# Reworked start, last 64 columns of the third layer on two column groups, and two more transposes on TensorE, in a convolution-and-MLP kernel written out task by task

## The chip, the cores and the metric

The kernel runs on one core of one Trainium2 chip. The metric is the device time in microseconds (us). Three runs of the kernel before took 302.81, 300.95 and 302.58 us; their median is 302.58 us. A core has a matrix engine (TensorE, PE in the profile; PEld is its loading of weights), VectorE (DVE), ScalarE (ACT), GpSimd (POOL), SyncE (SP, which here only issues transfers), and 16 DMA engines. Matmul results land in PSUM, from where VectorE or ScalarE copy them to SBUF ("eviction").

## The reference

One batch of S = 2048 positions with D = 640 channels; all inputs are bfloat16. `LN` is a layer norm without weights.

```
sa, ca, ga, sb, cb, gb = split(silu(c) @ w_mod)          # six vectors of 640
h   = LN(q) * (1 + ca) + sa
ksh = sum over t = 0..3 of shift(k, t) * shift_k[:, 3-t]  # causal, per channel
kv  = ksh * v
y   = irfft(rfft(kv, 4096) * rfft(ssm_k, 4096))[:2048] + kv * ssm_D
x   = q + ga * (h * y)
h   = LN(x) * (1 + cb) + sb
h1  = gelu(LN(h) @ w1)                                    # w1: 640 x 640
hs  = (quarters of h1 shifted by 1, -1, 2, -2 positions) @ w2
x1  = h + hs
x   = x + gb * (x1 + gelu(LN(x1) @ w3) @ w4)             # w3: 640 x 1728
```

## The kernel before, in words

**A plan written out by hand.** The body calls `add(engine, cost, function, r=..., w=...)` 1046 times. Each call records one task: a few instructions, with the regions of SBUF that it reads and writes, from which the dependences follow. The string `ORDER` (line 26 on) then lists each task by number with a letter for its engine (P, A, D, G, S for PE, ACT, DVE, POOL, SP) and, for tasks that take PSUM, the slot. `Planner.run` goes through this list, and each engine executes its tasks strictly in the listed order. The costs given to `add` play no part in the order; some tasks allow two engines, and the letter in `ORDER` decides. A transfer is issued by the queue that its letter names, in the order of that queue, so a transfer that must wait holds up those listed behind it.

**The front (0 to about 8 us).** `ssm_D`, `ssm_k` (five transfers of 128 channels, 512 KB each, into `Ra`, L228), `shift_k` and `c` are loaded in this order on SP. `ssm_D`, `shift_k` and `c` come with the channel on the partition: `Dcol` (L226), `skT` (L229) and `c_col` (L230), where `Dcol` and `c_col` are filled element by element, two bytes each. k and v come transposed by DMA (L233). VectorE computes index columns in sixteen tiny steps (`scol`, L262 to L279). Tables of sines follow: GpSimd makes an integer ramp, VectorE multiplies it by an index column (L292) and takes it modulo the period (L293), and ScalarE applies the sine (`sin_to`, L321); a second table goes through GpSimd (`angles_pool`, `turns_to`). L332 and L333 finish the matrix `F1bd`, L348 writes a negated part of the table `RG`, and SP copies parts of it to other partitions (L353, L354). GpSimd builds diagonal matrices from the taps of `shift_k` into `RQ` (L355) and computes silu of `c` (L380 on).

**Transforms (8 to about 110 us).** The long convolution is a Fourier transform of length 4096, split into 64 x 64. L444 adds `Dcol` to the first tap of `ssm_k` in `Ra`, `to_slots` (L394) transposes 32 x 32 blocks on VectorE, `stage1` (L407) multiplies by `F1bd` on TensorE, and its results are evicted by ScalarE (L207) or VectorE (L209). `stage2` (L427) is the second transform. The same is done for kv, after `k_shift` (L463, L468), which runs on the diagonal matrices. The modulation vectors come from w_mod (L487 to L510). `inverse1` multiplies the two spectra. For that it needs a copy with real and imaginary parts exchanged: four such "swap" buffers `KSY` are used in turn, each filled by transfers on SP and GpSimd (L613), read by VectorE (L617), and followed by matmuls (L628, L629). L576 copies a table from `RK` to `RH`. `inverse2` (L661) is the last transform, 32 x 32 tiles of the array, sixteen at a time.

**Layers (110 us to the end).** The positions are held as sixteen tiles A of 128. The groups of the first layers are `CG` = [0], [1], [2], then pairs [3,4] to [13,14], then [15]; those of the later layers are `MG` = [1], then pairs [2,3] to [14,15], then [0]. For each group:

- `chain_a` (L737, L740): gate times convolution, residual sum, and a square sum on ScalarE (L729) for the variance; `ln_finish` turns sums into mean and scale on GpSimd (L714 to L717), its first part on VectorE where `ORDER` says so.
- `chain_b` (L751, L756): modulation, and statistics of the next norm.
- `chain_c`: the norm itself (`normed`, L724 for the first groups, L592/L594 otherwise), then `turn`, which brings channels onto partitions: for the first `pe_c = 4` groups (tiles 0 to 4) with five transposes on TensorE (L772) and an eviction by ScalarE or VectorE (L778, L780), for the later ones by a transposing DMA on SP (L765). `pe_m = 3` says the same for the groups of the later layers.
- `mm_w1`: first layer (L818), gelu (L820), and its remaining 32 channels of each quarter (L828, gelu in four pieces on ScalarE, L834).
- `mm_w2`: mixing matmul (L873), residual on VectorE (L880), square sum, norm, turn.
- `mm_w3`: third layer (L907). The 1728 columns of w3 are 13 blocks of 128 and 64 left over. SBUF holds the left-over 64 twice (L1020, a copy on GpSimd), as a fourteenth block of 128 columns; so TensorE computes 14 blocks per group, in tasks of 4, 4, 4 and 2, each block five matmuls with the group's 128 or 256 positions as moving columns. gelu follows (L911).
- `mm_w4`: fourth layer (L937), 13 blocks whole, and the half block with `half` (L928): four matmuls of 64 rows each, two at a time on the two row groups of the array. The first tile uses the upper copy, the second the lower copy of the doubled 64.
- VectorE adds residuals and multiplies by gb (L960 to L966), and SP sends the output (L969).

The weights w1 and w2 are loaded at L992 to L995, w3 at L1012, w4 at L1014 and L1009/L1010, all on SP.

## Time and profile before

| view | value |
|---|---|
| median of three runs | 302.58 us |
| span of the profiled execution | 298.7 us |
| what lies around the span, taken from the median | 302.58 - 298.7 = 3.9 us |
| mean granted TensorE clock | 0.975 |
| TensorE matmuls, busy | 269.7 us, 90%, 3176 instructions |
| TensorE weight loads, busy | 208.5 us, 70% |
| VectorE, busy | 218.2 us, 73% |
| ScalarE, busy | 208.3 us, 70% |
| GpSimd, busy | 104.8 us, 35% |
| DMA | 35.76 MB in 58356 packets |

The profile is of one execution, and its rows are measured from the start of the span. The page gives no total for that execution besides its span, so the difference to the runs' median stands in the table as one term. Busy shares are means over stages: TensorE's 90% contains a stretch at the start where it has nothing to do and long stretches with no gap. The views used below are: the span cut into windows with the busy time of each engine; an engine's waits, each with the tile or line for which it waited (`PE ps_w L873 <- ACT R L820: 2.1, 1, 2.1` means that TensorE's matmuls of L873 waited in total 2.1 us, once, at longest 2.1 us, for ScalarE's L820); the timeline of one engine (start, duration, instruction, and in brackets the idle time before it with what ended it); the costliest groups of instructions; the transfers in slices; and the chain of work that ended last. A name such as `R` or `T` in a row is the buffer's name without its number.

### The profile page before, as it was taken

The numbers are of one execution on the slowest core, as the hardware profiler recorded it, in microseconds if no ns is written. First come the engines' busy times: TensorE is split into PE (matmuls) and PEld (weight loads), VectorE is DVE, ScalarE is ACT, GpSimd is POOL, SyncE is SP. The second block draws the span as 40 slices with busy tenths as digits, with TensorE's granted clock in tenths as the row PEclk, the third lists the DMA queues.
The fourth block names the chain that finished last, engine by engine and source line by source line (L and its number), as shares of the span: only waits on it lengthen the run. The fifth ranks groups of instructions, "written<-read, shape, count | busy, mean of one in ns | idle before, by whom it ended". The sixth has DMA issues, their size and how long they took to land.

```text
span 298.7 us, 7890 instructions
## 1 busy us (share of the span) xinstructions
PE 269.7 (90%) x3176; PEld 208.5 (70%) x3182; DVE 218.2 (73%) x438; ACT 208.3 (70%) x341; POOL 104.8 (35%) x237
## 2 busy tenths in 40 slices
PE   0999999999989766869999999999999999999993
PEld 0666755777878436648878677787788767887871
DVE  8998999999999998898759589886361544212442
ACT  4799989999999789979868775766854705431200
POOL 5864364453216591434275426120421321100000
PEclk9999999999999859799999999999999999999999
DMA  6999999898999920563700203223113030510112
GB/s 215 275 215 184 225 137 246 225 217 221 229 253 281 280 65 2 153 203 69 273 4 0 46 5 68 56 46 60 41 40 80 5 89 6 63 43 23 29 52 60
DMA packets 58356, 35.76 MB, mean 120 GB/s; under 512 B 40032, under 2 KB 55008, under 8 KB 58320
## 3 DMA queue, kind: packets, MB, share of 16 engines
q1 hardware_dynamic: 57136, 32.01, 46.3%
q0 software_dynamic: 1088, 3.21, 4.1%
q8 instruction: 25, 0.41, 0.6%
q14 instruction: 11, 0.09, 0.1%
q10 hardware_dynamic: 96, 0.04, 0.1%
HBM read 16.31 MB, written 2.62 MB: 63 GB/s over the span
## 4 chain that ended last, share of the span: by engine, by line
PE 51%; DVE 13%; ACT 11%; DMA 10%; POOL 6%; issue 5%; SPq 2%; DVEq 0%; POOLq 0%; ACTq 0%
PE ps_w L937 17%; PE ps_w L907 14%; ACT T L207 5%; DMA Ra<-in_A_q_dram 5%; PE ps_w L873 4%; PE ps_w L818 3%; PE ps_s L427 3%; ACT RG L729 3%; DVE Rb L617 3%; PE ps_ksh L463 2%; POOL lnv L715 2%; PE ps_s L407 2%; DMA RK<-R 2%; DVE R L756 2%; PE ps_mod L493 2%
## 5 line engine op out<-in xcount | busy, mean ns | idle before, releaser
L907 PE MATMUL ps_w<-R,T 128*128 128x256 bf16 (+1 forms) x630 | 63.8, 261 | 0.7 <-DMA R<-RH 0.7
L907 PEld LDWEIGHTS <-T 128*128 128x128 bf16 x630 | 55.5, 98 | 7.9 <-issue 2.0
L937 PE MATMUL ps_w<-T,R 128*128 128x320 bf16 x416 | 59.1, 299 | 0.0
L911 ACT ACTIVATE R<-ps_w 128x1024 bf16<-128x1024 f32 (+2 forms) x36 | 28.8, 827 | 41.9 <-PE ps_w L907 41.9
L937 PEld LDWEIGHTS <-R 128*128 128x128 bf16 x416 | 40.5, 98 | 15.2
L960 DVE TENSOR_TENSOR T<-ps_w,R 128x640 bf16<-128x640 f32 x15 | 12.3, 822 | 35.4 <-PE ps_w L928 18.1
L207 ACT CAST T<-ps_s 128x1024 bf16<-128x1024 f32 x32 | 30.4, 1029 | 3.2 <-PE ps_s L407 3.1
L207 ACT CAST R<-ps_s 128x960 bf16<-128x960 f32 (+1 forms) x35 | 30.8, 964 | 1.8 <-PE ps_s L427 1.6
L407 PE MATMUL ps_s<-F1bd,Rb 128*128 128x256 bf16 x160 | 23.3, 298 | 8.7 <-DVE Rb L394 8.1
L729 ACT ACTIVATE RG<-R 128x640 bf16<-128x640 bf16 x32 | 23.5, 734 | 9.9 <-DVE R L880 6.7
L407 PEld LDWEIGHTS <-Rb 128*128 128x128 bf16 x160 | 16.7, 107 | 14.7 <-DVE Rb L394 8.6
L873 PE MATMUL ps_w<-RG,R 128*128 128x320 bf16 x160 | 23.2, 299 | 2.1 <-ACT R L820 2.1
L715 POOL TENSOR_TENSOR lnv<-lnv,mhalf 128x2 f32<-128x2 f32 (+1 forms) x29 | 22.5, 775 | 2.3
L427 PE MATMUL ps_s<-T,RG 64*128 64x160 bf16 x512 | 21.2, 230 | 0.8 <-ACT R L207 0.6
L880 DVE SCALAR_TENSOR_TENSOR R<-ps_w,R 128x640 bf16<-128x640 f32 x16 | 12.9, 819 | 11.8 <-PE ps_w L873 11.6
L427 PEld LDWEIGHTS <-RG 64*128 64x128 bf16 x512 | 17.7, 94 | 5.1 <-issue 4.6
L818 PE MATMUL ps_w<-R,RG 128*128 128x256 bf16 (+1 forms) x200 | 20.0, 259 | 1.3 <-DMA R<-RK 0.6
L873 PEld LDWEIGHTS <-R 128*128 128x128 bf16 x160 | 15.4, 98 | 8.2 <-ACT R L820 2.4
L629 PE MATMUL ps_i<-EB,Rb 128*128 128x128 bf16 x160 | 19.0, 219 | 1.5 <-DVE Rb L617 1.4
L818 PEld LDWEIGHTS <-RG 128*128 128x128 bf16 x200 | 17.1, 102 | 3.5 <-issue 2.0
L628 PE MATMUL ps_i<-EA,Rb 128*128 128x128 bf16 x160 | 19.0, 219 | 0.4 <-ACT R L207 0.3
L714 POOL TENSOR_TENSOR lnv<-stat,lnv 128x2 f32<-128x2 f32 x19 | 4.0, 212 | 40.9 <-ACT RG L729 28.7
(178 smaller groups left out, 513.5 us busy)
## 6 DMA issues: line engine op xcount, KB each, us to landing
Ra<-in_A_ssm_k_dram SPq DMA_DIRECT2D x5, 512.0 KB, 5.7
R<-in_w_mod_dram SPq DMA_DIRECT2D x6, 400.0 KB, 6.0
out_dram<-RH SPq DMA_DIRECT2D x60, 40.0 KB, 1.6
T<-in_B_w_dram SPq DMA_DIRECT2D x5, 432.0 KB, 6.2
RH<-in_w_mod_dram SPq DMA_DIRECT2D x4, 400.0 KB, 4.4
Ra<-in_A_q_dram SPq DMA_DIRECT2D x4, 320.0 KB, 6.6
RK<-R SPq DMA_DIRECT2D x5, 256.0 KB, 4.5
RK<-R POOLq DMA_DIRECT2D x5, 256.0 KB, 5.3
```

The lines of the kernel that those rows point to most:

```text
L207: nc.scalar.copy(dst, src(ps.tile))
L407: nc.tensor.matmul(psv[:, ml, :], lhsT=xL[:, s0:s0 + P], rhs=F1r, start=True, stop=True)
L427: nc.tensor.matmul(psv[:, g, j], lhsT=Gs[p, k, 64 - 64 * cc:192 - 64 * cc], rhs=T1h[h][p, cc * 32 + k], start=(cc == 0), stop=(cc == 1), t ...
L628: nc.tensor.matmul(psv[:, w, :], lhsT=Av[:, r_, :, g_], rhs=EAf, start=True, stop=False)
L629: nc.tensor.matmul(psv[:, w, :], lhsT=Bv[:, r_, :, g_], rhs=EBf, start=False, stop=True)
L715: nc.gpsimd.tensor_tensor(rs, rs, mhalf[:, 0:n], ALU.pow)
L729: add("ACT", 0.74, lambda e: nc.scalar.activation(junk, src, ACT.Square, scale=float(D) ** -0.5, accum_out=stat[:, li, 1, t:t + 1]), r=[sk ...
L818: nc.tensor.matmul(pt[:, fb, 0:cw], lhsT=w1_sb[:, b, 160 * fb:160 * fb + P], rhs=hT[:, b, 0:cw], start=(b == 0), stop=(b == ND - 1))
L873: nc.tensor.matmul(pt[:, hf, 0:320], lhsT=gsf[:, fb, c0:c0 + P], rhs=w2_sb[:, fb, 320 * hf:320 * hf + 320], start=(fb == 0), stop=(fb == 4))
L907: nc.tensor.matmul(pt[:, fl, 0:cw], lhsT=w3_sb[:, b, fb * P:(fb + 1) * P], rhs=xT[:, b, 0:cw], start=(b == 0), stop=(b == ND - 1))
L911: nc.scalar.activation(g3[g % 2][:, f0:f0 + fn, 0:cw], ps.tile[:, 0:fn, 0:cw], ACT.Gelu_apprx_tanh)
L937: nc.tensor.matmul(bank(i, hf), lhsT=gg[:, fb, i * P:(i + 1) * P], rhs=w4_sb[:, fb, 320 * hf:320 * hf + 320], start=(fb == 0 and i == 0), ...
```

## The change

Five things are changed together.

1. **Front with rows.** `ssm_D`, `c` and `shift_k` are loaded with five rows on five partitions (contiguous pieces) into the first part of `T01`. A small unit matrix `eye` is made on GpSimd, and TensorE turns the rows into columns with tiny matmuls: one for `ssm_D`, five for `c` and the four taps. ScalarE copies the results to `Dcol` and to `csk`, which holds `c_col` and `skT`. A sine of one column runs early on ScalarE. Of the sixteen tiny index steps nine stay on VectorE, and six (with one merged) go to GpSimd. For the first sine table the multiplication by the index column (L292) moves from VectorE to ScalarE (two activations of 128 x 512), the modulo stays. The negation of L348 may now run on ScalarE. `diagw` has its two inner axes exchanged.
2. **Exchanged swap buffers.** The third and the fourth of the four swap buffers `KSY` change places: the third is now the part of `Rb`, the fourth the second half of `RK`.
3. **Tiles 5 and 6 turned on TensorE.** `pe_c` becomes 5: the group [5,6] gets ten transposes and two evictions (L772, L778/L780) in place of two transposing DMAs (L765).
4. **Half block on two column groups.** The fourteenth block of the third layer is computed with 64 weight columns at a time: for a group of two tiles, column group 0 takes the first tile's 128 positions, column group 1 the second's, so that ten matmuls of 128 columns replace five of 256. For a group of one tile both column groups take the same 128 positions, and ten matmuls of 128 columns replace five of 128. The result is 128 columns wide in PSUM in both cases, so gelu and `half` read 128 columns. The copy on GpSimd that doubled the 64 columns goes.
5. **A new `ORDER`.** It lists 1056 tasks. TensorE's tasks keep their order, but for neighbours that change places. These tasks move to another engine: L444 for the second and fourth block of channels (GpSimd to VectorE); one eviction of the modulation matmuls (ScalarE to VectorE); one eviction of kv's first transform (VectorE to ScalarE); an eviction of the last transform for tiles 11 to 13 (ScalarE to VectorE); the copies after three turns (first layer's tile 2, later layers' tiles 1 and 2: ScalarE to VectorE); the first part of `ln_finish` of the later layers' first group (GpSimd to VectorE) and of its second group (VectorE to GpSimd); the norm of tile 4 (VectorE to ScalarE); the first norm's statistics of tile 15 (ScalarE to VectorE) and of tile 8 (VectorE to ScalarE); two norms of q, tiles 9 and 15 (VectorE to ScalarE); and some of the norms and `ln_finish` parts of later groups. On ScalarE the four gelu pieces (L834) of the group [2] move behind the square sum (L729) of tile 3. The transfers of the third swap are issued ahead of the table copies (L576) on SP and GpSimd. The mixing matmul (L873) of a further tile stands ahead of the transposes that wait for L724. The loads of w4 no longer stand behind two transposing DMAs on SP.

```diff
 ORDER = """
...
-    KSY = [(RG[:, 6144:8192], ("RG", 6144, 8192)), (RK[:, 0:2048], ("RK", 0, 2048)), (RK[:, 2048:4096], ("RK", 2048, 4096)), (Rb[:, 8192:10240], ("Rb", 8192, 10240))]
+    KSY = [(RG[:, 6144:8192], ("RG", 6144, 8192)), (RK[:, 0:2048], ("RK", 0, 2048)), (Rb[:, 8192:10240], ("Rb", 8192, 10240)), (RK[:, 2048:4096], ("RK", 2048, 4096))]
...
-    dma("SP", 8, lambda q: ld_tiny(q, Dcol[:], A_ssm_D.rearrange("(b p) -> p b", p=P)), w=[("Dcol", 0, 1)], rate=8.0)
+    dma("SP", 8, lambda q: q.dma_start(rowD, A_ssm_D.rearrange("(b p) -> b p", p=P)), w=[("T01", 0, P)])
     for b in range(ND):
         dma("SP", 512, lambda q, b=b: q.dma_start(sT[:, b, :], A_ssm_k[b * P:(b + 1) * P, :]), w=[("Ra", 2048 * b, 2048 * b + 2048)], rate=390.0)
-    dma("SP", 8, lambda q: q.dma_start(skT[:], A_shift_k.rearrange("(b p) j -> p b j", p=P)), w=[("skT", 0, 1)], rate=30.0)
-    dma("SP", 8, lambda q: ld_tiny(q, c_col[:], c.rearrange("o (b p) -> p (o b)", p=P)), w=[("ccol", 0, 1)], rate=12.0)
+    dma("SP", 8, lambda q: q.dma_start(rows, A_shift_k.rearrange("(b p) j -> b (p j)", p=P)), w=[("T01", 2 * P, 6 * P)])
+    dma("SP", 8, lambda q: q.dma_start(rowc, c.rearrange("o (b p) -> (o b) p", p=P)), w=[("T01", P, 2 * P)])
...
+    def f(e):
+        nc.gpsimd.tensor_scalar(s64t[:], s64[:], 1.0 / 8192, None, ALU.mult)
+        nc.gpsimd.tensor_scalar(offc[:, 2:3], offi[:, 0:1], s64t[:], 0.5, ALU.mult, ALU.mult)
+        nc.gpsimd.tensor_scalar(offc[:, 3:4], offc[:, 2:3], 0.25, None, ALU.add)
+        nc.gpsimd.tensor_scalar(s32o[:], s32[:], 2.0 / 8192, 1.0 / 8192, ALU.mult, ALU.add)
+        nc.gpsimd.tensor_scalar(offc[:, 4:5], offi[:, 1:2], s32o[:], 0.5, ALU.mult, ALU.mult)
+        nc.gpsimd.tensor_scalar(offc[:, 5:6], offc[:, 4:5], 0.25, None, ALU.add)
+    add("POOL", 1.0, f, r=[("scol", 0, 1)], w=[("scolt", 0, 1)])
...
+    def f(e):
+        pt = pst(psD, name="ps_row")
+        nc.tensor.matmul(pt[:, 0, 0:ND], lhsT=rowD, rhs=eye[0:ND, :], start=True, stop=True)
+    add("ACT", 0.1, lambda e: nc.scalar.activation(lnv[:, 2, 0:1], b_pos[:], ACT.Sin), r=[("consts", 0, 1)], w=[("lnsp", 0, 1)])
...
+    t1 = add("ACT", 0.2, lambda e: nc.scalar.copy(Dcol[:], psD.tile[:, 0, 0:ND]), w=[("Dcol", 0, 1)], use=psD)
...
             def f(e, m_=m_, off=off):
-                nc.vector.tensor_scalar(m_, ti, s_col, off, ALU.mult, ALU.add)
+                if not split:
+                    nc.vector.tensor_scalar(m_, ti, s_col, off, ALU.mult, ALU.add)
                 nc.vector.tensor_single_scalar(m_, m_, q - 1, ALU.bitwise_and)
+            if split:
+                add("ACT", 0.25 + 0.00095 * n, lambda e, m_=m_, off=off: nc.scalar.activation(m_, ti, ACT.Identity, scale=s_col, bias=off),
+                    r=[keys[0], ("scol", 0, 1)], w=[k_])
...
-        add(("POOL", "DVE"), {"POOL": 1.48, "DVE": 0.35}, lambda e, k2s=k2s: eng_of[e].tensor_scalar(Gs[:, k2s, 128:192], Gs[:, k2s, 0:64], -1.0, None, ALU.mult),
-            r=[wk[:3]], w=[wk], port=0.4)
+        def f(e, k2s=k2s):
+            if e == "ACT":
+                nc.scalar.mul(Gs[:, k2s, 128:192], Gs[:, k2s, 0:64], -1.0)
+            else:
+                eng_of[e].tensor_scalar(Gs[:, k2s, 128:192], Gs[:, k2s, 0:64], -1.0, None, ALU.mult)
+        add(("POOL", "DVE", "ACT"), {"POOL": 1.48, "DVE": 0.35, "ACT": 0.65}, f, r=[wk[:3]], w=[wk], port=0.4)
...
-    pe_c, pe_m = 4, 3
+    pe_c, pe_m = 5, 3
...
+                    if fb == NF - 1:
+                        for b in range(ND):
+                            for i in range(2):
+                                c0 = P * i if cw > P else 0
+                                nc.tensor.matmul(pt[64 * i:64 * i + 64, fl, 0:P], lhsT=w3_sb[:, b, fb * P:fb * P + 64], rhs=xT[:, b, c0:c0 + P],
+                                                 start=(b == 0), stop=(b == ND - 1), tile_position=(0, 64 * i))
+                        continue
                     for b in range(ND):
                         nc.tensor.matmul(pt[:, fl, 0:cw], lhsT=w3_sb[:, b, fb * P:(fb + 1) * P], rhs=xT[:, b, 0:cw], start=(b == 0), stop=(b == ND - 1))
...
-            nc.tensor.matmul(bank(i, hf), lhsT=gg[p, NF - 1, i * P:(i + 1) * P], rhs=w4_sb[p, NF - 1, 320 * hf:320 * hf + 320],
+            nc.tensor.matmul(bank(i, hf), lhsT=gg[p, NF - 1, 0:P], rhs=w4_sb[p, NF - 1, 320 * hf:320 * hf + 320],
                              start=start, stop=stop, tile_position=(64 * k, 0))
...
-    def f(e):
-
-        nc.gpsimd.tensor_copy(w3_sb[:, :, F:FP], w3_sb[:, :, F - 64:F])
-    add("POOL", 0.6, f, w=[("T01", 0, ND * FP)])
```

149 lines of the change are left out of this document (82 added, 67 removed).

## The prediction

> **What bounds the kernel now.** I read the page first, for the span and the chain that ends last (TensorE holds half of it), then busy time by stage, then TensorE's waits, then the chain and the timeline of single engines.
>
> ```profile
> span 298.7 us, 7890 instructions
> ```
>
> The stages say more than the page's shares. Columns: the stage and its length, busy us of PE, PEld, DVE, ACT and POOL with their instructions, then TensorE's clock, DMA share, GB/s.
>
> ```profile
> 0.00:8.12 8.12, 0.00 (x1) 0.01 (x1) 6.96 (x31) 3.15 (x5) 4.80 (x15) 1.00 0.67 232
> 8.12:25.80 17.68, 17.22 (x104) 11.56 (x107) 17.25 (x19) 16.05 (x19) 10.13 (x8) 1.00 1.12 226
> 66.00:91.20 25.20, 23.02 (x428) 20.65 (x428) 24.98 (x25) 24.99 (x31) 5.95 (x12) 1.00 0.95 235
> 104.00:120.00 16.00, 11.40 (x269) 8.26 (x269) 14.72 (x39) 14.55 (x32) 8.84 (x25) 0.71 0.18 39
> 120.00:134.00 14.00, 10.48 (x177) 7.81 (x174) 12.37 (x37) 12.68 (x30) 6.05 (x19) 0.89 0.60 190
> 134.00:140.30 6.30, 5.72 (x85) 5.17 (x85) 4.87 (x14) 5.56 (x15) 2.61 (x7) 1.00 0.26 53
> 140.30:206.60 66.30, 65.04 (x551) 52.06 (x552) 51.30 (x129) 47.69 (x91) 25.35 (x66) 1.00 0.26 66
> 206.60:298.70 92.10, 87.39 (x758) 68.21 (x758) 34.79 (x79) 35.17 (x61) 11.95 (x38) 0.99 0.21 43
> ```
>
> Three regimes are to be seen. Until 8.12 us TensorE has nothing to do. From there to 91 us TensorE, VectorE and ScalarE are all full (24.98 and 24.99 of 25.20 us in the third row), so an earlier start moves everything, and work given to one of them is paid. From 104 to 134 us none is full: a chain of short normalisation steps goes round VectorE, ScalarE and GpSimd, and TensorE's clock is 0.71 to 0.89. From 134 us TensorE is full and what it has left sets the end. So a microsecond of TensorE work taken out behind 134 us is worth one, and so is each by which that full stretch begins earlier. TensorE's waits after 120 us, all of them (total, times, longest):
>
> ```profile
> PE ps_w L873 <- ACT R L820: 2.1, 1, 2.1
> PE ps_tr L772 <- DVE RH L724: 1.2, 2, 0.7
> PE ps_tr L772 <- ACT Rb L207: 0.7, 1, 0.7
> PE ps_w L907 <- DMA R<-RH: 0.7, 1, 0.7
> PE ps_w L818 <- DMA R<-RK: 0.6, 1, 0.6
> ```
>
> **The change, part by part.** The sum is made against the profiled execution, span 298.7 us. The runs have a median of 302.58 us, so I take 302.58 - 298.7 = 3.9 us around the span, unchanged.
>
> **Front with rows.** First the DMA view of the first 12 us (40 slices of 0.3 us) and of the first 3.5 us, then the chain, then VectorE's and ScalarE's timelines:
>
> ```profile
> GB/s 0 0 0 0 0 0 1 1 1 83 83 96 328 423 410 423 355 369 382 382 396 437 423 410 396 423 423 423 290 133 277 410 423 400 261 276 127 288 290 291
> DMA packets 672, 0.07 MB, mean 19 GB/s; under 512 B 656, under 2 KB 656, under 8 KB 672
> 1.32 4.08 DMA Ra<-in_A_ssm_k_dram
> ...
> 5.54 0.44 POOL Ra L444
> ...
> 18.43 7.31 ACT T L207 x8
> 2.41 0.21 DVE L274 TENSOR_SCALAR offc<-offi,s 128x1 f32<-128x1 f32 x1
> 4.93 0.54 DVE L292 TENSOR_SCALAR R<-R,s,offc 128x512 int32<-128x512 int32 x1
> 5.50 0.43 DVE L293 TENSOR_SCALAR R<-R 128x512 int32<-128x512 int32 x1
> 6.01 3.96 DVE L394 STREAM_TRANSPOSE Rb<-Ra 128x1024 int32<-128x1024 int32 x2
> 9.87 0.74 DVE L348 TENSOR_SCALAR RG<-RG 128x512 bf16<-128x512 bf16 x1
> 5.96 1.34 ACT L321 ACTIVATE RG<-R,b_pos 128x512 bf16<-128x512 int32 x2 [1.30 <-DVE R L293]
> ```
>
> 656 of the 672 packets before 3.5 us are under 512 B: the single elements of Dcol. Ra's first 512 KB, issued behind them, come at 1 to 96 GB/s until 3.6 us, then at about 400, and land at 1.32 + 4.08 = 5.40. With five row descriptors in Dcol's place the full pace could begin about 1 us sooner: landing at about 4.4 (estimate). VectorE must be ready as well. It loses two angle multiplications (0.54 each), the negation (0.74) and seven tiny steps. Its index column should be ready at about 2.4, as the row at 2.41 is now the eleventh of sixteen such steps. Dcol then waits on ScalarE behind two activations of 0.67 (1.34 for two) and comes at about 4.0. So the addition goes at about 4.5, the transpose (3.96 for two) ends at 6.7, and the first matmul follows at 6.8: 1.3 us sooner. The six tiny steps given to GpSimd cost at most 0.44 each by L444's row, 2.6 us; they delay the second angle table, but VectorE's part of that table comes later still, so this is hidden. ScalarE's additions lie before its first eviction, where it is busy 3.15 of 8.12 us. In the full stretch, one eviction of the second transform moves from VectorE to ScalarE (0.91 by the row of eight, 7.31) and a small copy the other way: some 0.5 us more on ScalarE, less on VectorE; I charge 0.3. Carried to 97 us: **-1.0** (ends 0, if Ra lands no sooner, and -1.3).
>
> **Exchanged swap buffers.** The third swap no longer waits for the table copies out of RK, but VectorE, its reader, is idle only 0.2 us in all between 66 and 91.2. Its issues on SP and GpSimd go ahead of the table copies, which wait there for TensorE anyway. The fourth swap takes the late place, with two multiplications more of time. **0** (ends -0.2 and +0.5).
>
> **Order behind the front.** TensorE's order is the old one but for neighbours that change places; what moves is the split of work between 110 and 140 us. ScalarE's timeline, and VectorE's next wait:
>
> ```profile
> 119.33 1.09 ACT L834 ACTIVATE R<-ps_w1x 32x128 bf16<-32x128 f32 x4
> ...
> 121.79 0.73 ACT L729 ACTIVATE RG<-R 128x640 bf16<-128x640 bf16 x1
> 124.07 0.80 DVE L594 TENSOR_SCALAR RK<-R,lnv 128x640 bf16<-128x640 bf16 x2 [1.15 <-POOL lnv L717]
> ```
>
> The square sum at 121.79 gates the statistics on GpSimd for which VectorE idles 1.15 us, and so tiles 3 and 4. In the new order the 1.09 us of L834 go behind it. ScalarE also gives VectorE an eviction and two transposed copies, which fit into such idle time, and takes a norm, which stands behind two activations and eats part of what was won. The 2.1 us wait for L820 keeps its place and its cause. I take **-1.1** (ends -2.3, both gains whole, and +0.9, the eviction not fitting). The longer wait of L772 for L724 now stands behind a further tile of the mixing matmul: **-0.7** (ends -0.7 and 0).
>
> **Tiles 5 and 6 turned on TensorE.** Ten transposes and two copies come, two transposes by DMA go:
>
> ```profile
> 136.24 2.60 SPq L765 DMA_TRANSPOSE R<-RK  x2
> 149.90 3.40 PE ps_w L937 x25
> ...
> 155.83 0.57 PE ps_tr L772 x10
> ```
>
> Ten transposes take 0.57, and TensorE is full there: **+0.6**. The two copies lie where VectorE and ScalarE have slack (4.87 and 5.56 of 6.30 us). On SP the loads of w4 no longer stand behind the 2.60 us of issue and the wait before it; TensorE has no wait for them today, so 0. Of the two waits for later transposes by DMA (0.7 and 0.6), one has fewer output transfers ahead of it on SP: **-0.3** (ends -1.3 and 0).
>
> **Half block on two column groups.** Four stages: a task of two blocks with 256 columns, the same with 128, the four half matmuls that share the array by row groups today, and 96 matmuls on sixteen small tiles.
>
> ```profile
> 162.77:163.87 1.10, 1.10 (x13) 0.98 (x11) 1.06 (x3) 1.10 (x3) 0.25 (x2) 1.00 0.00 0
> 136.86:137.42 0.56, 0.56 (x14) 0.56 (x11) 0.53 (x3) 0.36 (x1) 0.00 (x0) 1.00 0.00 0
> 242.67:243.05 0.38, 0.38 (x5) 0.12 (x6) 0.00 (x0) 0.00 (x0) 0.00 (x0) 1.00 1.11 217
> 96.91:98.04 1.13, 1.13 (x97) 0.95 (x96) 1.13 (x4) 0.79 (x2) 1.05 (x2) 1.00 1.05 329
> ```
>
> The half block is five matmuls of 256 columns now, half of 1.10: 0.55. It becomes ten of 128 columns in pairs on two column groups. If pairs overlap they stream like five of 128 columns, half of 0.56: 0.28. What regrouping costs is seen at the row groups: a matmul of 320 columns takes 0.136 (3.40 for 25), so two pairs 0.27, but the four took 0.38: 0.1. So 0.38, a gain of 0.17 in seven groups of two tiles and a loss of 0.1 in two of one tile, where ten matmuls replace five: -1.2 + 0.2. **-0.9**, by the row-group row, the nearest in kind. One end is no cost of regrouping (-1.9). The other is the pace of the small tiles: 1.13 / 96 = 11.8 ns on sixteen tiles is 188 ns for each matmul of one tile, five rounds are 0.94, and 7 x 0.39 + 2 x 0.66 = +4.1. The evictions get shorter and GpSimd's copy that doubled the half block goes; neither is waited for, 0.
>
> The Trainium skill, TensorEngine Tiling (Array Packing), says under Key Properties that changing the tiling mode drains TensorE, and under Restrictions and Gotchas that column tiling excludes Fast Weight Load. The first agrees with the 0.1 above and leaves the sum where it is; the second speaks against the edit, and by it the term would lie nearer the small tiles' end, at worst 304.2 us. No row here has column groups of 64 that could decide.
>
> Sum: -1.0 - 1.1 - 0.7 + 0.6 - 0.3 - 0.9 = -3.4; 298.7 + 3.9 - 3.4 = 299.2 us, 1.1% below the median.
>
> **The rivals.** (1) The gain is swallowed: VectorE and ScalarE bound the chain up to 134 us, the new split gives nothing (0 for -1.1 and -0.7) and the front carries 0.6. For it: they are busy 12.37 and 12.68 of 14 us there. Against it: the idle 1.15 us in one piece. -0.6 + 0.6 - 0.3 - 0.9 = -1.2: 301.4 us. (2) Slower: column groups do not hide their weights. At the small tiles' pace +4.1 stands for -0.9, so -3.4 + 5.0 = +1.6: 304.2 us. For it: nothing but that pace. Against it: the row groups, whose weight loads took 0.12 of 0.38 us. It turns the sign from about 0.55 + 2.5 / 9 = 0.83 us for such a half block. (3) More than summed: the front carries whole, the waits on DMA go and regrouping is free: -1.3 - 1.1 - 0.7 + 0.6 - 1.3 - 1.9 = -5.7, 296.9 us. (4) The half block does not do what it says: its pairs run one after the other, 0 for -0.9: 300.1 us.
>
> **How the numbers follow.** About 1% (3 us) is what a measurement of this kernel can tell from no change. Chances: the sum or near it (298.0 to 300.5) 0.45; rival 1 0.17; rival 2 0.10; rival 3 0.13; rival 4 0.08; a stall that I did not see in the new order, beyond 305.6, 0.07. Faster by over 1% means below 299.55: two thirds of the first, rival 3, and a little of rival 4, 0.46. Slower by over 1%: the stall and the upper half of rival 2, 0.12. Within 1%: 0.42. The range 296.0 to 304.0 leaves out the stall, the worse half of rival 2 and the best of rival 3, under 2 in 10.
>
> **What would show each step.** First matmul near 6.8 us with Ra's first landing near 4.4: the front. TensorE full from about 131 instead of 134 us: front and order. The last task of a group of two tiles in about 0.93 us instead of 1.10: the half block; 1.10 is rival 4, above 1.35 rival 2. No wait of TensorE over 0.7 us behind 140: the turns. I am wrong if the first matmul moves and the full stretch does not.

## The result and the profile after

The changed kernel has a median of 300.06 us (22 runs, 299.27 to 303.52), the kernel before beside it 302.27 us (22 runs, 300.66 to 304.39). The ratio is 0.9945, 95% interval 0.9925 to 0.9965: 0.55%, by the ratio about 1.7 us faster (the two medians differ by 2.2), where 3.4 us were forecast. The direction is right and the time lies in the range, but the gain is half as large and below the 1% that the prediction named as the least that can be told from no change.

The first line of the changed kernel's page, and its stages, with the columns as before:

```profile
span 299.1 us, 8023 instructions
```

```profile
0.00:8.12 8.12, 1.47 (x8) 1.02 (x9) 6.49 (x25) 5.54 (x11) 6.80 (x20) 1.00 0.72 258
8.12:25.80 17.68, 17.22 (x130) 11.45 (x132) 16.63 (x19) 16.73 (x22) 9.83 (x10) 1.00 1.05 208
66.00:91.20 25.20, 22.69 (x414) 19.88 (x412) 24.69 (x25) 24.49 (x30) 6.08 (x12) 1.00 0.90 225
104.00:120.00 16.00, 12.53 (x311) 8.92 (x311) 15.09 (x40) 14.19 (x31) 9.71 (x26) 0.52 0.24 52
120.00:134.00 14.00, 11.24 (x198) 9.26 (x196) 13.51 (x35) 12.92 (x31) 7.77 (x17) 0.94 0.66 199
134.00:140.30 6.30, 5.72 (x86) 4.95 (x85) 5.93 (x17) 4.52 (x11) 2.82 (x8) 1.00 1.04 324
140.30:206.60 66.30, 65.84 (x588) 52.38 (x586) 52.21 (x138) 52.17 (x99) 21.83 (x58) 1.00 0.19 34
206.60:298.70 92.10, 87.60 (x784) 66.93 (x781) 34.52 (x77) 34.29 (x60) 13.26 (x40) 1.00 0.21 43
```

The span is longer than that of before (298.7) although the kernel is faster. This profiled execution took 300.78 us, so 1.7 us lie around its span. With the same 1.7, the profiled execution of before took 300.4 us, 1.9 us under its median. The prediction's 3.9 us "around the span" were thus 1.7 us and the luck of a quick execution. In the stages, two things are seen at once: between 140.3 and 206.6 us TensorE is busy 65.84 us instead of 65.04, so its waits there are nearly gone; and from 134 to 140.3 us the DMA share is 1.04 instead of 0.26, so the loads of w4 run earlier.

The front, by TensorE's, VectorE's and ScalarE's timelines of the changed kernel:

```profile
2.31 0.18 PE L291 MATMUL ps_row<-T 5*128 5x5 bf16 x1 [2.31 <-DMA T<-in_A_ssm_D_dram]
6.83 1.89 PE L441 MATMUL ps_s<-F1bd,Rb 128*128 128x256 bf16 x8 [4.34 <-DVE Rb L428]
```

```profile
4.53 0.16 DVE L478 TENSOR_TENSOR Ra<-Ra,Dcol 128x1 bf16<-128x1 bf16 x1 [0.29 <-DMA Ra<-in_A_ssm_k_dram]
```

```profile
3.69 0.14 ACT L294 CAST Dcol<-ps_row 128x5 bf16<-128x5 f32 x1
```

`Dcol` is there at 3.83, the first 512 KB of `Ra` end VectorE's wait at 4.53 and the first matmul starts at 6.83: forecast were 4.0, 4.5 and 6.8. What TensorE waits for from 120 us on:

```profile
PE ps_w L906 <- ACT R L853: 1.5, 2, 1.3
PE ps_w L947 <- DVE R L813: 0.6, 1, 0.6
PE ps_w L851 <- ACT R L867: 0.5, 1, 0.5
PE ps_w L851 <- DMA R<-RK: 0.5, 1, 0.5
```

L853 is the L820 of before: its wait is 1.3 us instead of 2.1. The waits for transfers behind 140 us, 0.7 and 0.6 before, are one of 0.5.

Since single executions differ by some 2 us, the place of a gain is read from starts of the same TensorE task in several traces (us; the two kernels are means of two traces each, the second ones from the first experiment below, and every other row is one trace):

| kernel | first matmul | 2nd transform | inverse | tile 1, layer 1 | turn, 2nd later group | last group, layer 3 |
|---|---|---|---|---|---|---|
| before | 8.11 | 37.77 | 86.86 | 122.36 | 141.10 | 280.19 |
| changed | 6.96 | 36.85 | 87.47 | 123.96 | 140.80 | 278.57 |
| front alone | 7.03 | 36.69 | 85.67 | 121.12 | 140.25 | 279.63 |
| all but the front | 8.14 | 37.91 | 87.71 | 124.14 | 141.39 | 278.54 |
| half block undone | 7.01 | 36.77 | 87.33 | 123.04 | 139.98 | 277.01 |
| old middle | 6.88 | 36.90 | 86.36 | 122.24 | 139.59 | 276.69 |
| old middle, second trace | 7.05 | 40.22 | 90.00 | 125.78 | 142.73 | 279.85 |

So the changed kernel leads by 1.15 us at the first matmul, is 0.6 us late at 87 and 1.6 us late at 122 us, is 0.3 us ahead again at 141 and 1.6 us ahead near the end. Four stretches, then, are to be explained: a loss of 1.5 us between 38 and 87, a further 1.0 to 122, a gain of 1.9 from there to 141 and of 1.3 behind it. The two traces of before agree within 0.1 us at 38 us, but lie 0.6 us apart at 122, 1.6 at 141 and 2.8 near the end. Behind 100 us the table therefore shows the sense of a difference of 1 us, and not its size.

### The profile page after: what moved, and what is told of

Same layout as the page of the kernel before. It is cut to its first block, busy times and chain, and to the rows that moved or that the text cites. A ratio compares the mean times of both kernels' runs of the same rounds, so it can differ in the third digit from the quotient of the medians.

```text
span 299.1 us, 8023 instructions
## 1 busy us (share of the span) xinstructions
PE 272.5 (91%) x3237; PEld 208.9 (70%) x3243; DVE 218.0 (73%) x439; ACT 212.3 (71%) x347; POOL 105.6 (35%) x235
## 4 chain that ended last, share of the span: by engine, by line
PE 72%; ACT 15%; DVE 5%; issue 3%; DMA 3%; POOL 1%; SPq 1%; DVEq 0%; ACTq 0%
PE ps_w L947 20%; PE ps_w L982 18%; ACT T L208 8%; PE ps_w L906 7%; PE ps_w L851 5%; PE ps_ksh L497 5%; PE ps_s L441 5%; PE ps_s L461 4%; ACT R L208 2%; PE ps_mod L527 1%; PE ps_w1x L861 1%; DVE R L210 1%; DMA R<-RK 1%; PE ps_i L694 1%; PE ps_w L943 1%
## 5 line engine op out<-in xcount | busy, mean ns | idle before, releaser
L947 PE MATMUL ps_w<-R,T 128*128 128x256 bf16 (+1 forms) x585 | 61.0, 261 | 0.6 <-DVE R L813 0.6
L947 PEld LDWEIGHTS <-T 128*128 128x128 bf16 x585 | 51.1, 98 | 7.9 <-issue 1.8
L956 ACT ACTIVATE R<-ps_w 128x1024 bf16<-128x1024 f32 (+2 forms) x29 | 25.4, 886 | 28.3 <-PE ps_w L947 27.6
L208 ACT CAST T<-ps_s 128x1024 bf16<-128x1024 f32 x33 | 31.4, 1031 | 3.4 <-PE ps_s L441 3.2
L748 POOL TENSOR_TENSOR lnv<-lnv,mhalf 128x2 f32<-128x2 f32 (+1 forms) x29 | 23.1, 795 | 2.3
L851 PE MATMUL ps_w<-R,RG 128*128 128x256 bf16 (+1 forms) x200 | 21.0, 267 | 1.0 <-ACT R L867 0.5
L851 PEld LDWEIGHTS <-RG 128*128 128x128 bf16 x200 | 18.1, 106 | 3.0 <-issue 1.5
L497 PE MATMUL ps_ksh<-R,RQ 128*128 128x512 bf16 x74 | 18.2, 380 | 0.7 <-issue 0.5
```

Of the source, the lines that this page charges most:

```text
L208: nc.scalar.copy(dst, src(ps.tile))
L497: nc.tensor.matmul(pt[:, i, :], lhsT=diagw[:, b, jj, :], rhs=kT[:, b, c0:c0 + 512], start=(jj == 0), stop=(jj == 3))
L748: nc.gpsimd.tensor_tensor(rs, rs, mhalf[:, 0:n], ALU.pow)
L851: nc.tensor.matmul(pt[:, fb, 0:cw], lhsT=w1_sb[:, b, 160 * fb:160 * fb + P], rhs=hT[:, b, 0:cw], start=(b == 0), stop=(b == ND - 1))
L947: nc.tensor.matmul(pt[:, fl, 0:cw], lhsT=w3_sb[:, b, fb * P:(fb + 1) * P], rhs=xT[:, b, 0:cw], start=(b == 0), stop=(b == ND - 1))
L956: nc.scalar.activation(g3[g % 2][:, f0:f0 + fn, 0:cw], ps.tile[:, 0:fn, 0:cw], ACT.Gelu_apprx_tanh)
```

## The experiments

**Both kernels once more, for the scatter.** No edit.

> The changed kernel once more, for a second trace and for times on this chip. Theory A (what the trace shows of the stretch from 104 to 122 us is a property of the order): TensorE again stands at half clock for about 17 us there and the span is near 299.1 us. Theory B (the clock's windows lie at random to the program): the time at half clock changes by steps of about 3.4 us between executions, from 10 to 20 us, and the span moves with it between 297.6 and 301.8 us.

> The kernel before once more. Its profiled execution has a span of 298.7 us; with the 1.7 us that lie around the span of the changed kernel's profiled execution (300.78 - 299.1) it took about 300.4 us, less than nearly all of its 22 runs (median 302.27). Theory A (the profiled execution was a lucky one at the clock): a second trace shows a span of about 300.6 us with more than the 13 us at half clock of the first, and everything before 100 us at the same places within 0.1 us. Theory B (the first trace is typical, and more time lies around the span): span 298.7 us again and 3.6 us around it.

The changed kernel took 300.91 us (0.9949, 0.9923 to 0.9974), the one before 302.96 us (1.0002, 0.9975 to 1.0029). Between 100 and 137 us TensorE's clock is at half for 17.1 us in both traces of the changed kernel and for 13.7 us in both of before (10.2 and 3.4 us, in two pieces). So the first execution of before, 3.2 us shorter in span than the second, was not quick by a better clock. TensorE's waits behind 140 us in the second trace of before:

```profile
PE ps_w1x L828 <- DMA R<-RK: 1.0, 1, 1.0
PE ps_w L907 <- DMA R<-RH: 0.6, 1, 0.6
PE ps_w L818 <- DMA R<-RK: 0.6, 1, 0.6
PE ps_tr L772 <- DVE RH L724: 0.5, 1, 0.5
```

Waits for transfers are 2.2 us here, where the first trace had 1.3. The prediction's base was an execution in which they were short. In the changed kernel's second trace there is none of them behind 140 us.

**The front alone.** The new front on the old order, old swap buffers, old turns and old half block.

```diff
-    KSY = [(RG[:, 6144:8192], ...), (RK[:, 0:2048], ...), (Rb[:, 8192:10240], ...), (RK[:, 2048:4096], ...)]
+    KSY = [(RG[:, 6144:8192], ...), (RK[:, 0:2048], ...), (RK[:, 2048:4096], ...), (Rb[:, 8192:10240], ...)]
-    pe_c, pe_m = 5, 3
+    pe_c, pe_m = 4, 3
```

> Of the change only the front: rows, unit matrix, index steps, the angle multiplications on ScalarE; the order of the front up to the copy into the taps' column is the changed one, everything behind it is in the order of the kernel before, with its swap buffers, turns and half block. Theory A (the transposed loads of v set the pace): the first matmul goes at 6.8 us, the lead is 0.9 us at 35 us and falls to about 0.4 us where the third block of v arrives, near 38.5 us; 0.4 us faster than before. Theory B (the lead is carried whole, as predicted): 0.9 us at 97 us and 0.9 to 1.0 us faster. Theory C (the new order behind it lost the lead, not the loads): 0.9 us at 97 us here, against a lead of the changed kernel that is below zero at 50 us.

It took 303.87 us (1.0047, 1.0019 to 1.0075), but says nothing on the front: where the new front meets the old order, one PSUM slot was taken twice in a row, TensorE waits 1.13 us for it at 11.16 us, and by 19.57 us, where before stands at 19.38, the lead is gone. With the slots dealt out anew:

> Of the change only the front, as in the first such run, with the PSUM slots behind the front renamed so that the fourth matmul group takes the slot that the row matmuls have freed (in the first run it waited 1.13 us there, at 11.16 us). Theory A (the transposed loads set the pace between 35 and 50 us): the lead is 0.9 us at 35 us, VectorE waits longer for the third block of v, and at 57 us at most 0.3 us are left; total within 0.4 us of the kernel before. Theory B (the lead was lost to the new order of the stretch behind it): still 0.9 us at 57 us and at 97 us; 0.9 us faster.

302.48 us, 1.0025 (1.0001 to 1.0049). By the table the lead holds at 37.8 (1.1 us), 87 (1.2) and 122 us (1.2), and still the time is not better than before. Behind 122 us the lead is 0.85 us at 141 and 0.6 us at 280, although this execution is 1.3 us quicker than the kernel's median. One place where time is paid back, with the transfer that it waits for:

```profile
166.56 3.50 SPq L796 DMA_TRANSPOSE R<-RK  x2
```

```profile
171.58 2.34 PE L849 MATMUL ps_w<-R,RG 128*128 128x256 bf16 x20 [1.52 <-DMA R<-RK]
```

The group's first layer waits 1.52 us for a turn by DMA, where before it was 0.6 (L818). The transfer is not late against TensorE: it is issued 171.58 - 1.52 - 166.56 = 3.5 us before TensorE is ready for it, as in both traces of before. But its issue takes 3.50 us here, in both of those 2.54 us.

**All but the front.** The old front with everything else of the change.

> Everything of the change but the front: the order of the kernel before up to the third matmul group, the changed order, swap buffers, turns and column groups behind it. Theory A (the gain lies behind 100 us and owes nothing to the front): as fast as the changed kernel within 0.4 us, ratio to before near 0.995; no lead at 48 us, about 1.8 us gained from 122 to 140 us against the kernel before. Theory B (front and order only work together): no faster than before.

301.99 us, 0.9991 (0.9963 to 1.0019). So the front alone gives +0.25%, the rest alone -0.1%, both together -0.55%: inside the whole change the front is worth 0.9991 against 0.9946 (the changed kernel's two results together), 1.4 us, by the intervals 0.4 to 2.3. The parts do not add up. In the table this kernel is 0.85 us late at 87 and 1.8 us late at 122 us though it is level at 38 (37.91 against 37.77): the new order between 38 and 122 us costs by itself. (The row is of an execution 1.8 us quicker than this kernel's median, so its last columns say little.)

**Half block undone.** The changed kernel with the fourteenth block 128 columns wide, computed as before, and with the doubling copy on GpSimd.

```diff
-                    if fb == NF - 1:
-                        for b in range(ND):
-                            for i in range(2):
...
-                                nc.tensor.matmul(pt[64 * i:64 * i + 64, fl, 0:P], lhsT=w3_sb[:, b, fb * P:fb * P + 64], rhs=xT[:, b, c0:c0 + P],
-                                                 start=(b == 0), stop=(b == ND - 1), tile_position=(0, 64 * i))
-                        continue
+        nc.gpsimd.tensor_copy(w3_sb[:, :, F:FP], w3_sb[:, :, F - 64:F])
```

> The changed kernel with the fourteenth block of the third layer as before: 128 doubled columns, five matmuls, the copy on GpSimd that doubles them. Theory A (column groups work, and cost a little): the last task of a group of two goes from 1.11 back to 1.25 us in TensorE's row, that of a group of one from 0.84 to 0.72; 7 x 0.14 - 2 x 0.12 = 0.74 us slower than the changed kernel. Theory B (the predicted sizes, 0.17 and 0.1): 0.9 to 1.0 us slower. Theory C (the end is set elsewhere than on TensorE): the same time within 0.3 us.

299.70 us, 0.9920 (0.9889 to 0.9951): no worse than the changed kernel (0.9945, 0.9949). The last task of the third layer for a group of two tiles, then for one tile, in the changed kernel, and after it in this one:

```profile
163.68:164.72 1.04, 1.04 (x18) 0.70 (x15) 1.01 (x3) 0.84 (x1) 0.96 (x2) 1.00 0.00 0
257.46:258.25 0.79, 0.79 (x18) 0.60 (x16) 0.00 (x0) 0.79 (x2) 0.00 (x0) 1.00 0.00 0
```

```profile
162.43:163.52 1.09, 1.09 (x12) 0.97 (x10) 1.06 (x3) 0.89 (x1) 1.01 (x2) 1.00 0.00 0
255.55:256.11 0.56, 0.56 (x13) 0.56 (x11) 0.00 (x0) 0.56 (x2) 0.00 (x0) 1.00 0.00 0
```

With pairs the task takes 1.04 instead of 1.09 us for two tiles and 0.79 instead of 0.56 for one. Over seven groups and two that is 7 x -0.05 + 2 x 0.23 = +0.1 us: the edit gains nothing.

**What a half block costs in four forms.** In the changed kernel the half block of six groups takes another form: "serial" (all five matmuls of one column group, then those of the other), "wide" (pairs of 256 columns, so twice the work), "one" (a single column group with 256 columns, the half block of w4 then on one row group). The rest keep pairs of 128.

```diff
+    FORM = {2: "serial", 3: "wide", 4: "one", 5: "serial", 6: "wide", 7: "one"}
...
+                    if fb == NF - 1 and FORM.get(g, "pair") == "one":
+                        for b in range(ND):
+                            nc.tensor.matmul(pt[0:64, fl, 0:cw], lhsT=w3_sb[:, b, fb * P:fb * P + 64], rhs=xT[:, b, 0:cw],
+                                             start=(b == 0), stop=(b == ND - 1), tile_position=(0, 0))
+                        continue
```

> The changed kernel with other forms of the half block in single groups of two tiles, so that TensorE's rows price each form: group 1 as changed (pairs on two column groups in turn, 0.49 us measured for the five pairs), groups 2 and 5 all five matmuls of column group 0 and then all five of group 1, groups 3 and 6 pairs of 256 columns on both column groups (twice the work), groups 4 and 7 one column group of 64 with 256 columns, five matmuls, and the fourth layer's halves all on one row group. Theory L (each matmul pays its weight load, about 49 ns, and the streaming of the other group hides behind it): 0.49, then 0.56 or more, 0.55 and 0.55 us. Theory M (every change of column group costs some 40 ns on top of the streaming): 0.49, 0.60, 0.75 and 0.55 us. Theory S (the pairs run one after the other at 49 ns each, and nothing overlaps): 0.49, 0.49, 1.1 and 0.55 us.

The task in the forms pair, serial, wide and one, in this order:

```profile
143.21:144.25 1.04, 1.04 (x18) 0.70 (x15) 0.05 (x1) 1.04 (x3) 0.29 (x2) 1.00 0.00 0
162.33:163.46 1.13, 1.13 (x18) 0.79 (x15) 1.06 (x4) 0.93 (x1) 1.05 (x2) 1.00 0.00 0
194.42:195.72 1.30, 1.30 (x17) 0.86 (x14) 1.27 (x3) 0.00 (x0) 0.23 (x1) 1.00 0.61 121
205.55:206.85 1.30, 1.30 (x12) 0.85 (x10) 1.26 (x5) 0.00 (x0) 0.00 (x0) 1.00 0.00 0
```

Less the full block's 0.55 us, the half block takes 0.49, 0.58, 0.75 and 0.75 us. Wide pairs cost as much as one column group alone, 1.30, although they compute twice as much: the two column groups stream fully side by side. Even in the serial form they overlap: its starts are two chains of five, mostly 56 ns apart, the second beginning 85 ns after the first. What is left is a fixed price. Starts of single matmuls in the form "one" show where it lies (us, from the same trace):

```
last full matmul of 256 columns    205.984
first one of 64 weight columns     206.187   203 ns later (a matmul of 256 columns takes 109)
second one of 64 weight columns    206.320   133 ns later
...                                          109 ns apart
last one of 64 weight columns      206.648
next full matmul                   206.853   205 ns later
```

So 94 ns are lost on entering and 96 on leaving the stretch with column groups, and 24 between its first two matmuls: 0.21 us for each half block. In the form of the pairs, which follow each other every 56 ns, the same starts give 93, 99 and 24 ns, and 5 x 0.056 + 0.21 = 0.49 is what they measure. None of the expected forms of the cost was quite this: it is paid per regrouping, not per matmul or per weight load. By these longer tasks, and by fourth-layer tasks of 4.28 instead of 4.01 us where the half block of w4 is on one row group, this kernel does 2 x 0.09 + 2 x 0.26 + 2 x 0.26 + 2 x 0.27 = 1.76 us of TensorE work more than the changed one, and its time is 1.0004 (0.9973 to 1.0034) against 0.9946, 1.8 us more (0.7 to 2.8 by the intervals). That fits the prediction's premise that behind 134 us a microsecond of TensorE is a microsecond of time.

**TensorE's clock between 104 and 122 us.** In the changed kernel the clock is 0.52 from 104 to 120 us, in that of before 0.71. To see whether that holds the stretch up, the kernel with the half block undone got 28 dummy transposes in the turns of tiles 0 to 3 (nobody reads what they write; nothing else changes).

```diff
+    FILL = {(0, 0): 12, (1, 0): 4, (2, 0): 4, (3, 0): 8}
...
+            for _ in range(fill):
+                nc.tensor.transpose(pt[:, 1, 0, :], ident, ident)
```

> The changed kernel with the half block as before, and with transposes of the unit matrix in TensorE's waits ahead of the turns of tiles 0 to 3 (12, 4, 4 and 8 of them), whose results nobody reads. Theory A (the half clock costs time): the stretch at half clock between 102 and 122 us gets shorter by one or more steps of 3.4 us, to 10 us or less, and the time is 0.3 to 0.8 us below the run with only the half block undone (299.7 us there). Theory B (the norms on VectorE, ScalarE and GpSimd set that stretch, at either clock): the same time within 0.3 us, or 0.3 us more, because a turn waits for a filler that is still running.

299.75 us, 0.9929 (0.9904 to 0.9955), beside 0.9920 without them. The stretch in the kernel with fillers, then without:

```profile
104.00:122.00 18.00, 13.41 (x358) 10.27 (x357) 16.74 (x43) 16.28 (x36) 9.84 (x26) 0.77 0.16 35
```

```profile
104.00:122.00 18.00, 13.48 (x402) 10.57 (x372) 17.43 (x47) 16.24 (x36) 9.98 (x28) 0.72 0.17 38
```

In these two executions the half clock lasts equally long, 10.2 us, and only lies elsewhere: from 101.9 us with fillers and from 109.2 without. Over their runs the mean clock is 0.980 with fillers and 0.973 without: 0.007 x 298 / 0.5, about 4 us less at half clock, and no time for it. VectorE and ScalarE are busy 16 to 17 of the 18 us, so half clock there may lengthen matmuls that nobody waits for. This is not shown: the fillers may gain time and cost it elsewhere (the turn of tile 0 starts at 110.43 us without them and at 111.22 with them), and among the 22 runs of the changed kernel the ten with a clock below 0.973 took 301.5 us in the mean, the other twelve 299.8. Whether a low clock makes those long, or whatever makes them long lowers the clock, stays open.

**Old middle.** The new front, the old order and old swap buffers up to about 88 us, the changed order behind it, turns of tiles 5 and 6 on TensorE, the half block as before.

```diff
-    KSY = [(RG[:, 6144:8192], ...), (RK[:, 0:2048], ...), (Rb[:, 8192:10240], ...), (RK[:, 2048:4096], ...)]
+    KSY = [(RG[:, 6144:8192], ...), (RK[:, 0:2048], ...), (RK[:, 2048:4096], ...), (Rb[:, 8192:10240], ...)]
```

> The new front, then the order and the swap buffers of the kernel before up to about 88 us, then the changed order; turns of tiles 5 and 6 on TensorE, the half block as before. Theory A (the changed order itself loses the lead between 38 and 100 us, by waits for PSUM slots and by work put earlier on VectorE; behind 100 us it gains, whatever the lead): as with the front alone the lead over the first trace of before is near 0.8 us at 97 us, where the changed kernel is 1 to 2 us behind it, and the end comes 1.5 to 2 us earlier than with only the half block undone: about 297.9 us, ratio to before near 0.986. Theory B (the norms between 104 and 134 us swallow any lead): as with only the half block undone, ratio 0.990 to 0.994.

> The new front, the order of the kernel before up to about 88 us, the changed order behind, the half block as before, once more, since the first look had only six runs of it. Expected: 297.9 to 300 us, ratio to before 0.984 to 0.992, and again half a microsecond or less of the lead over the run with only the half block undone left at 140 us.

299.49 us, 0.9887 (0.9833 to 0.9942), and again 299.27 us, 0.9893 (0.9854 to 0.9932). It is the quickest version found: 1.1% below the kernel before. Weighted by their intervals, the two make 0.9891 +- 0.0032 and the two results of the changed kernel 0.9946 +- 0.0016, a difference of 0.55% +- 0.36%. Against the half block undone alone (0.9920, 0.9889 to 0.9951) the difference is not certain. In the table's first trace, of 1.0 us won by 87 us over the kernel with only the half block undone, 0.8 is left at 122 and 0.4 at 140 us. The second trace is of a long execution (301.47 us) and bears none of this out in its starts: it is 3.5 us behind the kernel with only the half block undone at 38 us, and 2.8 behind at 141. Its stretch from 38 to 87 us is nevertheless short, 49.8 us, beside 49.5 in the first trace, 49.1 before and 50.6 in the changed kernel.

**Tiles 5 and 6 by DMA again.** The changed kernel with `pe_c = 4`; the two transposing DMAs stand behind their norms, and so behind the loads of w4 on SP.

```diff
-    pe_c, pe_m = 5, 3
+    pe_c, pe_m = 4, 3
```

> The changed kernel with tiles 5 and 6 turned by transposing DMA again (issued behind the loads of w4 on SP). Theory A (the price as predicted): TensorE has 0.57 us of transposes less, no wait comes in their place, or one below 0.3 us; 0.3 to 0.6 us faster than the changed kernel. Theory B (the turns by DMA hold TensorE up, here or for the tiles behind them): a wait of L851 or of the third layer for a DMA of 0.5 us or more between 140 and 210 us, and the same time or up to 1 us more than the changed kernel.

303.22 us, 0.9999 (0.9965 to 1.0033): 1.6 us worse than the changed kernel. SP's and TensorE's timelines of this kernel, from an execution of 305.18 us, 2 us above its median:

```profile
129.23 2.98 SPq L1057 DMA_DIRECT2D T<-in_B_w_dram  x3
138.55 2.59 SPq L796 DMA_TRANSPOSE R<-RK  x2
```

```profile
145.13 0.71 PE L859 MATMUL ps_w1x<-R,RG 128*128 128x256 bf16 x5 [2.90 <-DMA R<-RK]
```

The loads of w4 keep the DMA engines busy, and the transposes issued at 138.55 behind them land 5.4 us after their issue; in the kernel before, where the same two go ahead of those loads, it is 2.6 us. TensorE waits 2.90 us. Of the waits for later turns by DMA one of 0.2 us is left. The new order with these two transposes ahead of the loads was not run.

**Tiles 5 and 6 on TensorE in the kernel before.** Ten transposes and two copies come, two transposing DMAs go; nothing else is changed.

```diff
-    pe_c, pe_m = 4, 3
+    pe_c, pe_m = 5, 3
```

> The kernel before with one part of the change: tiles 5 and 6 turned on TensorE, ten transposes between the first group's third layer and the next turns, near 139.6 us, the evictions on VectorE and ScalarE where they had no urgent work; everything else in the old order, the loads of w4 where they were. Theory A (the turns cost TensorE their 0.57 us, since the old order has no wait for those two tiles): 0.3 to 0.6 us slower than before. Theory B (the turns by DMA delay what stands behind them on SP, and the waits near 171, 207 and 235 us get shorter): the waits for a DMA behind 140 us, 1.3 to 2.2 us in the two traces of before, fall below 0.7 us, and the time is 0.3 to 1 us below before.

303.55 us, 1.0037 (1.0012 to 1.0063): 1.1 us slower. Its waits behind 140 us:

```profile
PE ps_w L817 <- DMA R<-RK: 1.2, 1, 1.2
PE ps_w1x L827 <- DMA R<-RK: 0.5, 1, 0.5
PE ps_tr L771 <- DVE R L779: 0.3, 1, 0.3
PE ps_w L906 <- DMA R<-RH: 0.2, 1, 0.2
```

They are 1.9 us in sum for transfers, no less than before. And the loads of w4 did not stay where they were, as the expectation had it: with the two transposes gone from SP's queue they are issued 13 us earlier (139.53 in the kernel before):

```profile
126.68 2.69 SPq L1013 DMA_DIRECT2D T<-in_B_w_dram  x3
```

So this kernel has both, the turns on TensorE and the early loads, and its waits for transfers stay. The same edit is a loss in the old order, and in the new one it is 1.6 us better than turns by DMA behind the loads.

## Why the prediction was half right

**The base.** It took 3.9 us around the span; 1.7 lie there. This changes no term, but the waits that the later terms were read from were short ones: 1.3 us for transfers behind 140 us in that execution, 2.2 in the next.

**Front, -1.0.** The start came as forecast (6.83 for 6.8, 6.96 in the mean of two traces). The step that failed is "carried to 97 us" and from there to the end. On the old order the front carries whole to 122 us and is then worth nothing (1.0025); in the new order the lead of 0.9 us at 37 us is a delay of 0.2 us at 58. Inside the whole change the front still is worth 1.4 us. So "an earlier start moves everything" holds for the full stretch in the old order and is not seen to hold beyond it. Where the lead goes behind 122 us stays open. The turns by DMA move with it, but they are issued only 3.5 us before TensorE is ready for them, and what such a short reserve costs differs between executions (0.6 and 1.5 us at the same place). That the lead counts once this reserve is longer, as in the new order, is an argument; a kernel with the front and nothing but a longer reserve was not run.

**Exchanged swap buffers, 0, and the order up to 122 us, not priced.** "TensorE's order is the old one but for neighbours that change places" left out 60 us of order. The new one loses some 1.5 us from 37 to 87 us; old middle shows it with the same front (86.36 against 87.33 in its first trace, and in both of its traces by the length of the stretch). Part of the place is seen in the changed kernel's TensorE timeline, where these waits are new:

```profile
38.34 1.90 PE L497 MATMUL ps_ksh<-R,RQ 128*128 128x512 bf16 x8 [0.48 <-issue]
42.29 0.59 PE L461 MATMUL ps_s<-T,RG 64*128 64x160 bf16 x12 [0.26 <-ACT R L208]
48.60 0.60 PE L441 MATMUL ps_s<-F1bd,Rb 128*128 128x256 bf16 x4 [0.40 <-ACT T L208]
```

With the front alone the second and third are not there, and the first is 0.31 us. Whether the swap buffers or the order of the evictions cost the rest was not taken apart.

**Order behind the front, -1.1 - 0.7.** Between tile 1's first layer and the turn of the second later group the changed kernel takes 140.80 - 123.96 = 16.84 us, that of before 18.74: -1.9. But between 87 and 122 us it takes 36.5 instead of 35.5: +1.0. The net is -0.9 with the ten added transposes in it, and about -1.5 without their 0.57, of -1.8 forecast. The wait for L820 kept its cause, as predicted, but not its length (2.1 to 1.3). The full stretch begins behind a last wait that ends at 136.57 us, not at 131; in the kernel before, by the same measure, it is 140.31. By its own sign ("I am wrong if the first matmul moves and the full stretch does not") the prediction is nearly wrong: the first matmul moved by 1.15 us, the turn of the second later group by 0.3. Two rows of TensorE's timeline, changed kernel:

```profile
132.82 2.89 PE L906 MATMUL ps_w<-RG,R 128*128 128x320 bf16 x20 [1.34 <-ACT R L853]
136.57 1.28 PE L947 MATMUL ps_w<-R,T 128*128 128x128 bf16 x20 [0.58 <-DVE R L813]
```

**Turns, +0.6 - 0.3.** In the old order the edit costs 1.1 us (0.4 to 1.9), which has the +0.6 inside it. The 0 for SP's queue holds there too: the loads of w4 go earlier, and nothing is gained. In the changed kernel they also go 11 us earlier, 128.58 instead of 139.53 (the DMA share from 140.3 to 206.6 us is 0.19 instead of 0.26), and there the waits for later turns by DMA fall from 1.3 and 2.2 us in the two traces of before to 0.5 and none. But tiles 5 and 6 alone brought the same early loads and kept 1.9 us of waits, so neither the turns on TensorE nor the early loads end them. What does can be read from the first turn by DMA that both kernels share, that of tiles 7 and 8. SP's and then TensorE's timeline, in the kernel before:

```profile
166.62 2.54 SPq L765 DMA_TRANSPOSE R<-RK  x2
```

```profile
170.72 2.34 PE L818 MATMUL ps_w<-R,RG 128*128 128x256 bf16 x20 [0.60 <-DMA R<-RK]
```

and in the changed one:

```profile
165.80 2.59 SPq L798 DMA_TRANSPOSE R<-RK  x2
```

```profile
170.92 0.72 PE L861 MATMUL ps_w1x<-R,RG 128*128 128x256 bf16 x5
```

Before, TensorE is ready at 170.72 - 0.60 = 170.12, 3.5 us after the issue. In the changed kernel it comes 5.1 us after it and does not wait. The 3.5 us stand in all traces with the old order here (both of before, both kernels with the front alone, the turns alone), with waits of 0.6 to 1.5 us at this place. The 5.1 us stand in both traces of the changed kernel, without the front and without the half block, and none of them waits here. So this wait ends by the new order, which has the norms of these tiles done earlier against TensorE; which of its moved tasks does it was not taken apart. The other wait that both traces of before have, 0.65 us at 206.59, ends for the prediction's reason: ahead of that turn SP issues three output transfers before (its turn goes at 203.88 us) and one in the changed kernel (202.13), so it goes 4.3 instead of 2.1 us before TensorE is ready. The term is thus mis-sized, -0.8 to -2.2 for -0.3, since the sum let the wait at 171 us stand, and its place is the order and not the turns. What the turns on TensorE do in the new order is something else: they keep tiles 5 and 6 from waiting behind the early loads of w4 (2.90 us).

**Half block, -0.9.** Measured +0.1 in tasks, and by time no gain (0.9920 without the edit, 0.9945 and 0.9949 with it; the intervals overlap). The pairs stream as forecast; the mis-sized term is the regrouping, taken as 0.1 us per half block from the row groups, where it is 0.21. With 0.21 a half block of two tiles takes 0.28 + 0.21 = 0.49 against 0.55, a gain of 0.06 (forecast 0.17, measured 0.05); one of one tile loses 0.21 (forecast 0.1, measured 0.23). The Trainium skill, TensorEngine Tiling (Array Packing), Key Properties, states that a change of tiling mode drains TensorE. The trace agrees, with 94 and 96 ns lost at the two ends of the stretch. The same page of the Trainium skill states under Restrictions and Gotchas that column tiling excludes Fast Weight Load. No cost of that shows here: weight loads of 64 columns take 110 ns instead of 98, but matmuls of 128 and 256 columns still follow each other every 56 and 109 ns. (The sum -1.2 + 0.2 in the prediction is -1.0 as written, and -0.92 with unrounded terms.)

**The rivals.** The time is that of rival 4 (300.1) and the mechanism is near to it and to rival 1: the half block does nothing, though its pairs do overlap, and part of the rest is swallowed ahead of 122 us. Rival 2's slow column groups did not come: wide pairs cost no more than a single column group. Rival 3's end of the waits on DMA did come, and covers part of the two misses, though by the new order and not by the turns.

## What to carry to other kernels

A transfer is priced by how far ahead of its need it is issued and by what stands ahead of it: a turn by DMA issued 5.1 us before TensorE needed it cost nothing, one issued 3.5 us before cost 0.6 to 1.5 us, and one behind bulk loads 2.90. Making the transfers behind it earlier is worth nothing if nobody waits for those. Before a gain is put down to one part of a change, look in the trace of the single-part run whether a second thing came with it. Splitting the array for a short tail pays only if what it saves exceeds the regrouping (0.21 us here), so count the stretches and not the columns. A sum made against one profiled execution inherits its luck: set the span against that execution's own time, and look at two executions before a wait of a microsecond is taken as a term.

## What the runs showed of the hardware

A change between full and 64-column matmuls costs 94 to 99 ns each way and 24 ns more behind the first, while matmuls on two column groups start 3 to 4 ns apart and then run fully side by side.

A tiny operation can be held for the whole length of one on another engine. In the two traces of old middle, VectorE's addition to one column of `Ra`, and GpSimd's selection over `RQ`; first the quick execution, VectorE then GpSimd:

```profile
9.64 0.16 DVE L477 TENSOR_TENSOR Ra<-Ra,Dcol 128x1 bf16<-128x1 bf16 x1 [0.65 <-DMA Ra<-in_A_ssm_k_dram]
```

```profile
9.70 2.47 POOL L388 TENSOR_SCALAR_AFFINE_SELECT RQ<-csk 128x2560 bf16<-128x2560 bf16 x1
```

and the slower one, 301.47 us against 298.31:

```profile
10.32 2.17 DVE L477 TENSOR_TENSOR Ra<-Ra,Dcol 128x1 bf16<-128x1 bf16 x1 [1.16 <-DMA Ra<-in_A_ssm_k_dram]
```

```profile
10.00 2.47 POOL L388 TENSOR_SCALAR_AFFINE_SELECT RQ<-csk 128x2560 bf16<-128x2560 bf16 x1 [0.25 <-ACT csk L303]
```

Where VectorE starts 0.06 us ahead it takes 0.16 us; where it comes 0.32 us behind, it ends at 12.49, as GpSimd does at 12.47, and 0.16 have become 2.17 us. The Trainium skill, SBUF — State Buffer, SBUF: two separate sides, states that the two engines share a pair of ports as an exclusive lock for a whole instruction, when VectorE's operation has two inputs in SBUF and GpSimd's reads SBUF; the rows agree. The slower trace is 0.7 us behind the quick one before this (TensorE at 9.64 against 8.97 us), 2.6 us behind after it (14.62 against 12.01) and 3.3 at 38 us, so its whole difference arises ahead of 38 us. Whether this race is what makes the other long runs of these kernels was not tried.
